# Full-array matmuls in four column parts, Q's masked copies in one op, and a fifth pair: a two-layer transformer block on one Trainium2 core

## The chip, the cores and the metric

The kernel runs on one core of a Trainium2 chip. The metric is the device time of one execution in microseconds (us); smaller is better. The kernel before takes 1614.82 us in the median of six runs (1612.02 to 1617.56). The engines of the core are called here as the profile calls them: PE (TensorE: matmuls; PEld is its loading of weights), DVE (VectorE), ACT (ScalarE), POOL (GpSimd) and SP (SyncE, which only issues DMAs here). Matmul results land in PSUM, of which the kernel uses eight banks of 128 partitions by 512 f32.

## The reference

```python
def _A_ref(x, wqkv, wo):                 # attention, 32 heads of 16
    qkv = (x @ wqkv).reshape(B, S, 3, H, Dh).transpose(2, 0, 3, 1, 4)
    q, k, v = qkv[0], qkv[1], qkv[2]
    scores = jnp.einsum("bhqd,bhkd->bhqk", q, k) * (Dh ** -0.5)
    p = _softmax(scores, axis=-1)
    o = jnp.einsum("bhqk,bhkd->bhqd", p, v)
    return o.transpose(0, 2, 1, 3).reshape(B, S, D) @ wo
...
x = x + _A_ref(_layernorm(x), A_wqkv, A_wo)
x = x + _B_ref(_layernorm(x), B_w1, B_w2)      # relu(x @ w1) @ w2
x = x + _A_ref(_layernorm(x), A_wqkv, A_wo)
x = x + _B_ref(_layernorm(x), B_w1, B_w2)
```

S is 2048, D 512, the hidden width of B 1792, and all inputs are bf16. The same weights serve both layers. With heads of 16 the scores are many and thin: 2 layers x 32 heads x 2048 x 2048, each of which wants one exp.

## The kernel before

**Tiles.** Queries go in chunks of 512 columns (QS); layer 1 takes its last two chunks as four of 256. Keys go in 16 blocks of 128 (kb). Eight heads lie in the 128 partitions of one key tile T, two heads in each strip g of 32 partitions. A unit of the attention is one head, one key block and one chunk of queries: a score matmul (L1302) with 32 contraction rows writes 128 keys x 512 queries into a PSUM bank. Since a strip holds two heads, Q exists in two copies, in each of which the other head's rows are zero; `q_masked` (L624 to L628) makes them out of a bank with one op for each e (0, 1). A score matmul uses the rows of one strip (tile position (32g, 0)), so that three of them, with different g, run beside each other.

**Slots.** Three banks (W = 3) form a slot: three units, three score matmuls side by side, and one exp on ACT over all three banks (L1311, 128x1536, bf16 result in one of five buffers `ebuf`). There are two sets of three banks (`ps_s`), one bank `ps_o` for the sums of values, and one, `ps_f`, for all other matmuls. The values' products (L901) contract 128 keys into 32 output rows: four of them, with different g, use the four column strips of the array (tile position (0, 32g)) and add into `ps_o`. A `vaug` block has a column of ones beside each head's values, so that the softmax sums come along; they are divided out later (L828 to L836).

**Pairs.** DVE computes some of the exps itself. In two slots, two apart, it takes the third bank instead of ACT, whose exp is then 128x1024 wide. `dve_block` (L991) copies such a bank as integers into half of a buffer `lin` (L995, step 1), and `chain` (L1031) works on both halves: bits kept (L1036), squared (L1047), bits kept again (L1036), multiplied (L1051; some pairs have one more step, L1048). The value products are then made three times, with `lin`, `step` and `cube`. There are NP = 4 buffers `lin` and NC = 3 of `step` and `cube`. A new pair begins only while fewer than NP are in flight, counted from the oldest that still has value products to make (L1200), and only where the planner's estimate of DVE's backlog (L1208) and of when its chain would end (L1207, L1217) allow it.

**The rest of the work.** Layer norm, K, Q, V, the output projection, and the two products of block B are groups of full-array matmuls, cut into pieces by `mm_group` (L418 to L441). A piece is one matmul of 128x128 weights by 512 or 256 columns (L434). When a group's last piece is out, DVE empties the bank: `k_fin`, `v_group`, `q_group`, `h_group` and others give the op. The transposes of layer norm (L516) are groups of a single piece with a cost of 1.3. Layer norm's reciprocal root is begun on DVE (`ln_rstd`, L473 to L480) and refined on POOL (`ln_newton`, L498 to L503), in buffers `va_`, `ya_`, `ta_` of which there are two of each.

**The order.** It is written by a planner in the kernel's own Python, which keeps a clock for PE and one for DVE. For each slot it places pieces of groups (`fill_pe`), rounds of value products (`fill_v`) and then the score matmuls (L1297 to L1307), before the time at which the exp before would end. If a slot has too little PE work, the score matmuls are issued again (`times`, L1293). `pe_start` (L257) adds SWITCH = 105 ns when the kind of PE work changes: "s" (scores), "v" (values), "f" (all else). The DVE queue is filled by `run_dve` in this rank: step 1 of a pair, emptying a bank, other tasks, chains. The order of each engine's instructions is thus fixed in the program. Q for the run after next is requested when a run's first unit comes up (L1181 to L1186) and lies in one of two buffers `qbuf`.

**Head and tail.** Before the first slot the first chunk's layer norm, K, Q and V are made with all engines (L1071 to L1117). After the last slot the last chunk's projection and block B remain (L1368 to L1438).

Of the kernel before, what the change touches and what calls it, by code (L numbers as in the profile page):

```python
# [24 lines left out]
def kernel(  # L25
# [41 lines left out]
    UNIT = 128.0  # L67
    EXP_BIAS = (127.0 - math.log2(SUM)) * UNIT
    CHAIN = 2500.0
    NP = 4  # L70
    NC = 3
    THIRD = (8, 9, 10, 11)

# [27 lines left out]
        return persist.tile(shape, dt, name=name)  # L101

    ident = sb([P, P], BF16, "ident")
    mask = [sb([P, 1], FP32, f"mask{e}") for e in range(2)]
    qmask = [sb([P, 1], FP32, f"qmask{e}") for e in range(2)]
    wqkv = sb([P, NDC, 3 * D], BF16, "wqkv")
    wo = sb([P, NDC, D], BF16, "wo")
    w1buf = [sb([P, NDC, P], BF16, f"w1_{n}") for n in range(NW1)]
# [38 lines left out]
    acc0 = [x[:].bitcast(FP32).rearrange("p a b -> p (a b)") for x in htp]  # L147
    acc0.append(kt1[:].bitcast(FP32).rearrange("p a b -> p (a b)"))
    ebuf = [sb([P, W * QS], BF16, f"e{n}") for n in range(NE)]
    qbuf = [[sb([P, QS], BF16, f"q{n}_{e}") for e in range(2)] for n in range(2)]  # L150
    ubuf = [sb([P, QS], FP32, f"u{n}") for n in range(NU)]
    rbuf = [sb([P, QS], FP32, f"r{n}") for n in range(NU)]
    cbuf = [sb([P, QS // 32], FP32, f"c{n}") for n in range(NU)]
    xnbuf = [sb([P, D], BF16, f"xn{n}") for n in range(TPC)]
    stats = [sb([P, nc.vector.BN_STATS_DIM], FP32, f"stats{n}") for n in range(2)]
    mv = [sb([P, TPC, nc.vector.BN_AGGR_DIM], FP32, f"mv{n}") for n in range(2)]
    va_ = [sb([P, TPC], FP32, f"va{n}") for n in range(2)]
    ya_ = [sb([P, TPC], FP32, f"ya{n}") for n in range(2)]
    ta_ = [sb([P, TPC], FP32, f"ta{n}") for n in range(2)]
    warm = sb([P, 1], FP32, "warm")  # L160

    ps_s = [psum.tile([P, W, QS], FP32, name=f"ps_s{n}") for n in range(2)]
# [80 lines left out]
    def at(keys, engine):  # L243
# [10 lines left out]
            t = max(t, when)  # L254
        return t

    def pe_start(kind, ready=0.0):  # L257
        return max(now_pe[0] + (SWITCH if mode[0] != kind else 0.0), ready)

    def pe_run(kind, units, ready=0.0):  # L260
        now_pe[0] = pe_start(kind, ready) + units * MM
# [38 lines left out]

    def do_piece():
        c, fn, ready = cur.popleft()
        pe_run("f", c, ready)
        fn()
        owed[0] -= c

# [111 lines left out]
    def mm_group(mms, fin, makes, deps, per=1, cost=EVAC, after=None, wide_by=QS, sums=1):  # L418


        hold = {}
        pieces = []
        n = len(mms)
        for a in range(0, n, per):

            def piece(a=a):
                if a == 0:
                    hold["b"] = bank()[:, 0 : sums * wide_by]
                b = hold["b"]
                for i in range(a, min(a + per, n)):  # L430
                    lhsT, rhs = mms[i]
                    k = n // sums
                    out = b[:, i // k * wide_by : (i // k + 1) * wide_by]
                    nc.tensor.matmul(out, lhsT, rhs, start=i % k == 0, stop=i % k == k - 1)  # L434
                if a + per >= n:
                    put_evac(cost, lambda: fin(b))
                    if after:
                        after()

            pieces.append((min(per, n - a) * wide_by / QS, piece))  # L440
        return group(pieces, makes, deps)  # L441
# [51 lines left out]
    def ln_newton(tag):  # L493

        n = ln_n(tag)
        a, y, t1 = va_[n][:], ya_[n][:], ta_[n][:]
        for _ in range(3):
            nc.gpsimd.tensor_mul(out=t1, in0=y, in1=y)  # L498
            nc.gpsimd.tensor_mul(out=t1, in0=t1, in1=a)
            nc.gpsimd.tensor_scalar(  # L500
                out=t1, in0=t1, scalar1=-0.5, scalar2=1.5, op0=ALU.mult, op1=ALU.add
            )
            nc.gpsimd.tensor_mul(out=y, in0=y, in1=t1)  # L503
# [117 lines left out]
            (wqkv[:, c, T * P : (T + 1) * P], xnT[xj][:, c, a : a + w]) for c in range(NDC)  # L621
        ]

    def q_masked(n, b, e, w=QS):  # L624
        return nc.vector.tensor_scalar(  # L625
            out=qbuf[n % 2][e][:, 0:w], in0=b, scalar1=qmask[e][:, 0:1], scalar2=None,
            op0=ALU.mult,
        )  # L628

    def q_group(n, l, j, T):  # L630
        xj, _, w = columns(l, j)
        cost = 133 + 1.045 * w

        def fin(b):
            q_masked(n, b, 0, w)
            evac.appendleft((cost, 0.0, lambda: (q_masked(n, b, 1, w), mark(("q", n)))))

        return mm_group(
            q_mms(l, j, T), fin, [("q", n)], each(TPC, "xnT", ("ln1", l, xj)), cost=cost,
            wide_by=w,  # L640
        )
# [151 lines left out]
    def finish_segment(sg, last):  # L793
        l, j, t, e = sg["l"], sg["j"], sg["t"], sg["e"]
        sums_wait[0] += 1
        if sg["store"] is not None:

            def store():
                if sg["load"] is not None:
                    nc.vector.tensor_add(out=sg["store"], in0=sg["load"], in1=ps_o[:])  # L800
                else:
                    nc.vector.tensor_copy(out=sg["store"], in_=ps_o[:])
                mark(("po",))
                sums_wait[0] -= 1

            musts.append((EVAC, now_pe[0] + PE_TO_DVE, store))
            return
        n = norm_no[0]
        norm_no[0] += 1
        if n >= NU:  # L810
            run_until(("m", n - NU))
        u, r, c = ubuf[n % NU], rbuf[n % NU], cbuf[n % NU]
        lane = DH if e == 0 else DH - 1
        width = sg["w"]
        at_column = columns(l, j)[1]
        sums = u[lane : P : 32, 0:width]
        c = c[:, 0 : width // 32]

        def copy():
            if sg["load"] is not None:  # L820
                nc.vector.tensor_add(out=u[:], in0=sg["load"], in1=ps_o[:])
            else:
                nc.vector.tensor_copy(out=u[:, 0:width], in_=ps_o[:, 0:width])  # L823
            mark(("po",))
            mark(("u", n))
            sums_wait[0] -= 1
            if sg not in segs[-2:]:
                nc.sync.dma_start(out=c, in_=sums)  # L828
                mark(("c", n), lag=C_LAG)

        musts.append((77 + 1.045 * width, now_pe[0] + PE_TO_DVE, copy))
        b = before(l, j)
        war = each(chunks[b][1], "o", *b) if b else []

        def mul(a, w):
            nc.vector.scalar_tensor_tensor(  # L836
                out=ot[t][:, at_column + a : at_column + a + w], in0=u[:, a : a + w], scalar=mask[e][:, 0:1],
                in1=r[:, a : a + w], op0=ALU.mult, op1=ALU.mult,
            )
            for i in range(a // P, (a + w) // P):  # L840
                mark(("ot", l, j, t, i))

        ended[l, j] = ended.get((l, j), 0) + 1
        quick = sg["load"] is not None or ended[l, j] == NT

        def recip():
            nc.vector.reciprocal(out=c, in_=c)
            nc.sync.dma_start(out=sums, in_=c)
            if not quick:
                nc.gpsimd.dma_start(  # L850
                    out=r[:, 0:width],
                    in_=bass.AP(
                        tensor=sums.tensor, offset=sums.offset,
                        ap=[list(sums.ap[0]), [0, 32], [1, width]],
                    ),
                )
            mark(("r", n), lag=U_LAG if quick else R_LAG)

        def spread():
            nc.vector.stream_shuffle(  # L860
                out=r[:, 0:width], in_=u[:, 0:width], mask=[lane] * 32
            )

        def spread_mul():
            if quick:
                spread()
            mul(0, width)

        def direct(i):
            if i == 0:  # L870
                spread()
            a = i * P
            nc.vector.reciprocal(out=r[:, a : a + P], in_=r[:, a : a + P])
            mul(a, P)

        def direct_all():
            for i in range(width // P):
                direct(i)

        ots = each(width // P, "ot", l, j, t)  # L880
        if last:
            last_steps.append(direct)
        elif sg is segs[-2]:
            task(3100, direct_all, ots + [("m", n)], war + [("u", n)])
        else:
            task(165, recip, [("r", n)], [("c", n)], place=0)
            cost = 105 + 1.1 * width + (200 + 1.05 * width if quick else 0)
            task(cost, spread_mul, ots + [("m", n)], [("r", n)] + war)
        if ended[l, j] == NT and not last:
            later = rest_of_chunk(l, j)  # L890
            work.extend(later)
# [180 lines left out]
    idle_matmuls(18)  # L1072
    for e in range(2):
        nc.vector.tensor_reduce(
            out=mask[e][:],
            in_=ident[:].rearrange("p (g e d) -> p e g d", g=4, e=2)[:, e],
            op=ALU.add, axis=mybir.AxisListType.XY,
        )
        nc.vector.tensor_scalar(
            out=qmask[e][:], in0=mask[e][:], scalar1=SCALE * LOG2E * UNIT, scalar2=None,  # L1080
            op0=ALU.mult,
        )
    for i in range(TPC):
# [24 lines left out]
    uses(nc.scalar.copy(out=ktp[0][0][0][:], in_=b), in_bank[0])  # L1108
    mark(("k", 0, 0, 0))
    b = plain(q_mms(0, 0, 0))  # L1110
    for e in range(2):
        uses(q_masked(0, b, e), in_bank[0])
    mark(("q", 0))
    for kb in range(2):
        b = plain(v_mms(kb))
# [57 lines left out]
    while units:  # L1173
# [123 lines left out]
        for _ in range(times):  # L1297
            pe_run("s", 1, s_ready)
            for a, (sg, kb, g) in sorted(zip(place, now), key=in_turn):
# [2 lines left out]
                nc.tensor.matmul(  # L1302
                    b[:, a : a + sg["w"]],
                    kt[32 * g : 32 * g + 32, kc : kc + P],
                    qbuf[sg["n"] % 2][sg["e"]][32 * g : 32 * g + 32, 0 : sg["w"]],
                    start=True, stop=True, tile_position=(32 * g, 0),
                )  # L1307
        m = len(now) - len(taken)
# [160 lines left out]
```

The softmax here doesn't subtract the row's maximum and nothing guards it: scores larger than these inputs give would overflow.

## Time and profile before

| | |
|---|---|
| profiled execution | 1614.79 us |
| its span in the profile | 1613.0 us |
| median of six runs | 1614.82 us |
| busy: ACT / DVE / PE | 1566.1 / 1496.7 / 1483.5 us |
| exps (L1311) | 1366 |
| step 1 of pairs (L995) | 662 |
| Q's masked copies (L625) | 102, and 2 in the head |
| value products (L901) | 6792 |
| full-array products (L434) in `ps_f` | 1576 |
| first exp starts, last exp ends | 16.7 us, 1578.1 us |
| granted clock of TensorE, mean | 0.998 |

The span runs from the first instruction to the last; the execution's own time is 1.8 us longer. A group in the profile is named by line, engine, operation and tiles (result <- operands, buffer numbers left out), then the shapes and the count; behind the bar stand the time in which at least one of its instructions ran, the mean duration of one in ns, and the idle time of the engine just before them with what ended it. Instructions of one engine overlap at their ends, so the distance between two starts is shorter than a duration. "x" before a number is a count. Line numbers are those of the kernel before.

### The profile page before, as it was taken

The page shows a single profiled execution, that of the slowest core. Times are in us where ns is not written, and L with a number is a line of the kernel's source. Part 1 is how long each engine was busy: PE and PEld are TensorE (multiplying, and loading weights), DVE is VectorE, ACT ScalarE, POOL GpSimd, SP SyncE. Part 2 cuts the span into 40 slices and gives each one's busy share as a digit, 9 for nine tenths or more (in the row PEclk, how much of TensorE's full clock was granted, in tenths as well). Part 3 has the DMA queues.
Part 4 walks back from the last instruction along what each step waited for, and adds up shares of the span by engine and source line. Part 5 has one row for each costly group of instructions (what it writes and reads, how often), then busy time and mean ns, then how long its engine had stood idle before and what let it go on. Part 6 is the DMA issues. An engine that isn't in the chain of part 4 may idle for free.

```text
span 1613.0 us, 35448 instructions
## 1 busy us (share of the span) xinstructions
PE 1483.5 (92%) x14863; PEld 508.6 (32%) x14863; DVE 1496.7 (93%) x3007; ACT 1566.1 (97%) x1387; POOL 94.0 (6%) x279
## 2 busy tenths in 40 slices
PE   8888889999999999999999999888999999999997
PEld 3222222322222222222222222222233333343444
DVE  7669999999999999999898998999999999999993
ACT  6999999999999999999999999999999999999993
POOL 2000001001010010000100000001001010010100
PEclk9999999999999999999999999999999999999999
DMA  5000000210002100021000100000110111021222
GB/s 164 1 1 2 2 2 8 47 28 10 7 15 44 25 15 8 12 48 25 9 1 17 30 1 1 2 3 10 43 30 16 27 28 38 19 49 37 47 48 70
DMA packets 113889, 39.97 MB, mean 25 GB/s; under 512 B 103328, under 2 KB 111264, under 8 KB 113728
## 3 DMA queue, kind: packets, MB, share of 16 engines
q1 hardware_dynamic: 101696, 26.21, 7.1%
q0 software_dynamic: 10688, 10.18, 3.4%
q8 instruction: 116, 1.90, 0.5%
q10 hardware_dynamic: 1344, 1.31, 0.2%
q14 instruction: 45, 0.37, 0.1%
HBM read 24.38 MB, written 2.10 MB: 16 GB/s over the span
## 4 chain that ended last, share of the span: by engine, by line
ACT 75%; PE 13%; DVE 8%; issue 3%; DMA 1%; ACTq 0%; DVEq 0%
ACT e L1311 75%; PE ps_s L1302 4%; PE ps_f L434 4%; PE ps_o L901 4%; DVE lin L995 2%; DVE step L1036 1%; DVE cube L1047 1%; PE ps_s L1365 1%; DVE cube L1051 1%; DVE stats L465 0%; DVE ot L836 0%; DVE x L708 0%; DMA w<-in_B_w_dram 0%; DVE ht L682 0%; DVE q L625 0%
## 5 line engine op out<-in xcount | busy, mean ns | idle before, releaser
L1311 ACT ACTIVATE e<-ps_s 128x1024 bf16<-128x1024 f32 (+1 forms) x1366 | 1555.0, 1370 | 6.8 <-PE ps_s L1302 4.9
L1302 PE MATMUL ps_s<-q,ktp 32*128 32x512 bf16 (+1 forms) x6060 | 600.6, 340 | 91.5 <-ACT e L1311 74.7
L901 PE MATMUL ps_o<-e,vaug 128*32 128x512 bf16 (+1 forms) x4284 | 495.1, 345 | 10.3 <-DVE u L823 4.8
L995 DVE TENSOR_SCALAR lin<-ps_s 128x512 int16<-128x512 f32 x662 | 451.3, 685 | 35.7 <-PE ps_s L1302 30.1
L1302 PEld LDWEIGHTS <-ktp 32*128 32x128 bf16 x6060 | 189.5, 91 | 505.1 <-issue 376.1
L1036 DVE TENSOR_SCALAR step<-lin 128x1024 int16<-128x1024 int16 x662 | 261.7, 418 | 3.3 <-PE ps_o L901 0.6
L901 PEld LDWEIGHTS <-vaug 128*32 128x32 bf16 x6004 | 161.6, 94 | 302.0 <-issue 291.1
L1047 DVE TENSOR_TENSOR cube<-step 128x1024 f16<-128x1024 bf16 x331 | 225.0, 683 | 2.7
L1051 DVE TENSOR_TENSOR cube<-cube,lin 128x1024 bf16<-128x1024 f16 x331 | 224.5, 679 | 0.0
L901 PE MATMUL ps_o<-step,vaug 128*32 128x512 bf16 (+1 forms) x836 | 143.1, 340 | 0.0
L901 PE MATMUL ps_o<-cube,vthird 128*32 128x512 bf16 (+1 forms) x788 | 138.1, 337 | 0.0
L901 PE MATMUL ps_o<-lin,vaug 128*32 128x512 bf16 (+1 forms) x836 | 127.4, 338 | 4.1 <-DVE u L823 2.8
L434 PE MATMUL ps_f<-xnT,w 128*128 128x512 bf16 (+1 forms) x496 | 126.8, 349 | 2.3 <-DVE ht L682 1.1
L434 PE MATMUL ps_f<-w,ht 128*128 128x512 bf16 x392 | 119.7, 384 | 0.9 <-DVE q L625 0.3
L850 POOL DMA_DIRECT2D r<-u x52 | 37.5, 722 | 1166.1 <-DVE step L1036 415.9
L434 PE MATMUL ps_f<-xnT,wqkv 128*128 128x512 bf16 (+1 forms) x328 | 92.0, 362 | 3.6 <-DVE ktp L575 0.5
L434 PE MATMUL ps_f<-wo,ot 128*128 128x512 bf16 x240 | 73.3, 387 | 0.5 <-DVE x L648 0.4
L682 DVE TENSOR_SCALAR ht<-ps_f 128x512 bf16<-128x512 f32 x103 | 70.5, 684 | 3.2 <-PE ps_f L434 3.0
L625 DVE TENSOR_SCALAR q<-ps_f,qmask 128x512 bf16<-128x512 f32 (+1 forms) x102 | 64.6, 659 | 2.9 <-PE ps_f L434 2.8
L434 PEld LDWEIGHTS <-w 128*128 128x128 bf16 x504 | 39.1, 97 | 60.0 <-issue 50.6
L836 DVE SCALAR_TENSOR_TENSOR ot<-u,mask,r 128x512 bf16<-128x512 f32 (+2 forms) x82 | 51.2, 626 | 1.1
L901 PEld LDWEIGHTS <-vthird 128*32 128x32 bf16 x788 | 39.8, 95 | 33.0 <-issue 30.3
(91 smaller groups left out, 612.1 us busy)
## 6 DMA issues: line engine op xcount, KB each, us to landing
w<-in_B_w_dram SPq DMA_DIRECT2D x140, 128.0 KB
r<-u POOLq DMA_DIRECT2D x25, 256.0 KB, 7.1
r<-u POOLq DMA_DIRECT2D x27, 128.0 KB, 4.5
out_dram<-x SPq DMA_DIRECT2D x16, 128.0 KB
x<-in_A_x_dram SPq DMA_DIRECT2D x14, 128.0 KB
w<-in_B_w_dram SPq DMA_DIRECT2D x1, 1792.0 KB
wqkv<-in_A_wqkv_dram ACTq DMA_DIRECT2D x2, 512.0 KB
c<-u SPq DMA_DIRECT2D x48, 8.0 KB
```

Source lines behind the costliest of these rows:

```text
L434: nc.tensor.matmul(out, lhsT, rhs, start=i % k == 0, stop=i % k == k - 1)
L625: return nc.vector.tensor_scalar(out=qbuf[n % 2][e][:, 0:w], in0=b, scalar1=qmask[e][:, 0:1], scalar2=None, op0=ALU.mult,)
L682: nc.vector.tensor_scalar(out=out, in0=sums, scalar1=0.0, scalar2=None, op0=ALU.max)
L836: nc.vector.scalar_tensor_tensor(out=ot[t][:, at_column + a : at_column + a + w], in0=u[:, a : a + w], scalar=mask[e][:, 0:1], in1=r[:, a ...
L850: nc.gpsimd.dma_start(out=r[:, 0:width], in_=bass.AP(tensor=sums.tensor, offset=sums.offset, ap=[list(sums.ap[0]), [0, 32], [1, width]],),)
L901: nc.tensor.matmul(ps_o[32 * g : 32 * g + 32, 0 : sg["w"]], values[:, 4 * sg["T"] + g, 2 * e : 2 * e + 32], rhs, start=g not in sg["begun" ...
L995: first = nc.vector.tensor_scalar(out=lin[which][:, half * QS : (half + 1) * QS], in0=src, scalar1=EXP_BIAS, scalar2=0.0, op0=ALU.add, op1 ...
L1036: nc.vector.tensor_scalar(out=stair, in0=line, scalar1=keep, scalar2=put, op0=ALU.bitwise_and, op1=ALU.bitwise_or,)
L1047: (609, lambda: nc.vector.tensor_mul(out=power, in0=mantissa, in1=mantissa)),
L1051: (609, lambda: nc.vector.tensor_mul(out=power.bitcast(BF16), in0=power, in1=line.bitcast(BF16))),
L1302: nc.tensor.matmul(b[:, a : a + sg["w"]], kt[32 * g : 32 * g + 32, kc : kc + P], qbuf[sg["n"] % 2][sg["e"]][32 * g : 32 * g + 32, 0 : sg[" ...
L1311: ex = nc.scalar.activation(out=eb[:, 0 : place[m]], in_=b[:, 0 : place[m]], func=ACTF.Exp, scale=1.0 / (LOG2E * UNIT),)
```

## The change

Five edits go together.

1. Each piece of `mm_group` issues its matmul as four, of 32 weight columns and 32 output rows each, at the tile positions that the value products use.
2. The planner's table of kinds (`MODE`) has "v" and "f" as one kind and gives the transposes a kind "t" of their own.
3. Q's two masked copies are one op: the bank read twice, times a [128, 2] tile of masks spread over the columns. Both copies lie in one tile `qbuf[n]`, both masks in one tile `masks`. Its estimated cost goes from two of 133 + 1.045 w to one of 90 + 2.09 w.
4. NP goes from 4 to 5: a fifth buffer `lin`, and a fifth pair in flight.
5. The two buffers of each of `va`, `ya` and `ta` become halves of one tile.

```diff
-    NP = 4
+    NP = 5
...
-    mask = [sb([P, 1], FP32, f"mask{e}") for e in range(2)]
-    qmask = [sb([P, 1], FP32, f"qmask{e}") for e in range(2)]
+    masks = sb([P, 4], FP32, "masks")
+    mask = [masks[:, e : e + 1] for e in range(2)]
+    qmask = masks[:, 2:4]
...
-    qbuf = [[sb([P, QS], BF16, f"q{n}_{e}") for e in range(2)] for n in range(2)]
+    qbuf = [sb([P, 2, QS], BF16, f"q{n}") for n in range(2)]
...
-    va_ = [sb([P, TPC], FP32, f"va{n}") for n in range(2)]
+    va2 = sb([P, 2, TPC], FP32, "va")
+    va_ = [va2[:, n] for n in range(2)]
...
+    MODE = {None: 0, "s": 1, "v": 2, "f": 2, "t": 3}
+
     def pe_start(kind, ready=0.0):
-        return max(now_pe[0] + (SWITCH if mode[0] != kind else 0.0), ready)
+        return max(now_pe[0] + (SWITCH if MODE[mode[0]] != MODE[kind] else 0.0), ready)
...
-        pe_run("f", c, ready)
+        pe_run("t" if c == 1.3 else "f", c, ready)
...
-                    nc.tensor.matmul(out, lhsT, rhs, start=i % k == 0, stop=i % k == k - 1)
+                    for g in range(4):
+                        cols = slice(32 * g, 32 * g + 32)
+                        nc.tensor.matmul(
+                            out[cols], lhsT[:, cols], rhs, start=i % k == 0,
+                            stop=i % k == k - 1, tile_position=(0, 32 * g),
+                            skip_group_check=True,
+                        )
...
-    def q_masked(n, b, e, w=QS):
-        return nc.vector.tensor_scalar(
-            out=qbuf[n % 2][e][:, 0:w], in0=b, scalar1=qmask[e][:, 0:1], scalar2=None,
-            op0=ALU.mult,
+    def q_masked(n, b, w=QS):
+        return nc.vector.tensor_mul(
+            out=qbuf[n % 2][:, :, 0:w],
+            in0=b.rearrange("p (e q) -> p e q", e=1).to_broadcast((P, 2, w)),
+            in1=qmask.rearrange("p (e q) -> p e q", q=1).to_broadcast((P, 2, w)),
         )
...
-        cost = 133 + 1.045 * w
+        cost = 90 + 2.09 * w
 
         def fin(b):
-            q_masked(n, b, 0, w)
-            evac.appendleft((cost, 0.0, lambda: (q_masked(n, b, 1, w), mark(("q", n)))))
+            q_masked(n, b, w)
+            mark(("q", n))
...
-                    qbuf[sg["n"] % 2][sg["e"]][32 * g : 32 * g + 32, 0 : sg["w"]],
+                    qbuf[sg["n"] % 2][32 * g : 32 * g + 32, sg["e"], 0 : sg["w"]],
```

`ya` and `ta` change as `va` does. The matmuls of the head (L1069, L1103), the transposes (L516) and the tail's own products (L1365) stay as they are.

## The prediction

> **What bounds the kernel now.** I read the page's chain first, then the groups by shape, then busy time by stage, and last the timeline of the engines around one slot. The chain, and the group that carries it:
>
> ```profile
> ACT 75%; PE 13%; DVE 8%; issue 3%; DMA 1%; ACTq 0%; DVEq 0%
> ...
> L1311 ACT ACTIVATE e<-ps_s 128x1024 bf16<-128x1024 f32 (+1 forms) x1366 | 1555.0, 1370 | 6.8 <-PE ps_s L1302 4.9
> ```
>
> ScalarE (ACT) runs 1366 exps that cover 1555.0 of the 1613.0 us, with 6.8 us idle before them. The other 58 us are the head (the first exp starts at 16.7), the tail (the last ends at 1578.1) and little else. So the time moves if the exps get fewer columns or start closer together. The groups by shape:
>
> ```profile
> L1311 ACT ACTIVATE e<-ps_s 128x1536 bf16<-128x1536 f32 x703 | 1053.5, 1577 | 4.3 <-PE ps_s L1302 2.6 <-PE ps_o L901 1.2
> L1311 ACT ACTIVATE e<-ps_s 128x1024 bf16<-128x1024 f32 x662 | 719.2, 1151 | 2.5 <-PE ps_s L1302 2.3 <-PE ps_o L901 0.2
> ...
> L995 DVE TENSOR_SCALAR lin<-ps_s 128x512 int16<-128x512 f32 x662 | 451.3, 685 | 35.7 <-PE ps_s L1302 30.1
> ```
>
> The 662 narrow exps are the slots whose third bank VectorE (DVE) takes at L995: 331 pairs. Neighbouring instructions overlap, so I price by distances between starts in the timeline: 1.330 us after a wide exp, 0.904 after a narrow one (medians). **One more pair saves 2 x 0.426 = 0.85 us of ACT.** All exps at these paces are 703 x 1.330 + 662 x 0.904 = 1533 us, while they span 1561: about 27 us are late starts. In the timeline 23 exps over 0.1 us late make 9.1 us of that; the rest is some 13 ns on nearly every exp, which I expect to stay.
>
> How much room has DVE for pairs? Busy time by stage (columns: window, PE, PEld, DVE, ACT, POOL, granted clock, DMA):
>
> ```profile
> 200.00:300.00 100.00, 89.16 (x785) 26.47 (x780) 95.34 (x189) 98.02 (x89) 4.74 (x14) 0.97 0.06 12
> ...
> 500.00:600.00 100.00, 93.96 (x773) 27.88 (x771) 98.24 (x190) 100.00 (x92) 4.73 (x11) 1.00 0.13 27
> ...
> 900.00:1000.00 100.00, 94.36 (x786) 29.36 (x783) 90.94 (x174) 99.63 (x89) 3.78 (x12) 1.00 0.03 8
> ```
>
> Best stages are 98% busy, the one at 900 only 91%. From 100 to 1560 us DVE is busy 1395.4 of 1460: 64.6 us are idle. That idle time, and what the change frees on DVE, is the purse.
>
> **All full-array products in four column parts.** The timeline of PE (start, us, line) shows both forms and the switch:
>
> ```profile
> 802.73 0.39 PE L901 MATMUL ps_o<-lin,vaug 128*32 128x512 bf16 x1
> 803.06 0.82 PE L434 MATMUL ps_f<-wqkv,xnT 128*128 128x512 bf16 x3
> 803.81 0.39 PE L1302 MATMUL ps_s<-q,ktp 32*128 32x512 bf16 x3
> ```
>
> ```profile
> 154.96 0.62 PE L901 MATMUL ps_o<-e,vaug 128*32 128x512 bf16 x8
> 155.40 0.39 PE L901 MATMUL ps_o<-lin,vaug 128*32 128x512 bf16 x4
> 155.72 0.39 PE L1302 MATMUL ps_s<-q,ktp 32*128 32x512 bf16 x3
> ```
>
> A value round followed by a full product takes 0.33 us from start to start. Full product to full product is (0.82 - 0.39) / 2 = 0.215. Two value rounds of four column products take 0.44, so 0.22 each, eight instructions included. A change of form thus costs about 0.105, and a full product cut in four should cost what a value round does. Following the rows of PE, a value round meets a full product 606 times one way and 65 the other: 671 x 0.105 = 70 us of PE go. L434 has 392 + 336 + 264 + 240 + 120 = 1352 wide products and 224 of 256 columns; at 0.01 us more for each that gives back at most 16 us. Transposes keep the full form; a cut product beside one now pays a switch, at most once for each of 64, 7 us. The planner's table MODE drops the same switch, so its order counts on it. The 3 x 1576 added products and as many weight loads are in that round price. PE is 92% busy, not the bound, so its 47 to 70 us reach the time only through late exps. 9.1 us are there to win; about 3 of them fall at 235 to 242 us, where the clock was granted at 0.5, and others are DVE's. I take 1.5 us; the ends are 0 and 9.
>
> No row shows four column products that read the same moving operand. The nearest is the value round, whose four read different blocks; its worst form, four after one another, is 3 x 0.215 more per wide product and half that for the others, 945 us in all. I take the value round, since shape, tile and bank use are the same.
>
> The Trainium skill, "TensorEngine Tiling (Array Packing)", section Restrictions and Gotchas, speaks against the edit: column tiling excludes Fast Weight Load. This trace does not show that as a price: the value products' weight loads last 94 ns on average against 97 for full ones, and whole rounds keep 0.22 us. If the four loads ran one after another instead, a product would take 4 x 0.094 = 0.38 us and the edit would cost 1576 x 0.16 = 250 us of PE; by the rounds it costs nothing.
>
> **Q's masked copies in one op.** Today two TENSOR_SCALARs at L625 (two start at 17.11 us and last 1.41 together: 0.66 from start to start), 0.40 each for the 256 form. The new op reads 1024 elements. L823 takes 683 ns for 512 and 417 for 256 elements of f32, 1.04 ns per element; a two-operand op of 512 (L648, 681) holds DVE for 0.60, so one of 1024 holds it 0.60 + 0.53 = 1.13. For 256 columns it is 0.60. Saved: 1.32 - 1.13 = 0.19, and 0.20. With 51 runs: 51 x 0.19 = 9.7 us of DVE. Ends: at the slope of L836 (747 and 468, 1.09 per element, start distance 0.67) it is 1.22, saving 5 us; at the rate of the 16-bit L1047 (1024 in 0.60) it would save some 31. The source is f32 in PSUM, so I take 9.7. A pair costs DVE 2 x 0.60 (L995) + 2 x 0.33 (L1036) + 0.60 (L1047) + 0.60 (L1051) = 3.06. So 9.7 / 3.06 = 3.2 pairs, **-2.7 us**, where the planner spends it on pairs. The single op delays a step 1 queued behind it on DVE by up to 1.13 instead of 0.66, 51 times; the scores wanted next are two slots ahead, so I price that in the third rival. In the head the first scores wait for both copies, but stand behind L434 at 15.53 anyway: nothing.
>
> **A fifth pair.** A pair holds its lin buffer from its first L995 to its last L901 product on cube. Counted so, pairs live 13.8 us in the median, 4 are in flight for 31% of 100 to 1560 us, 3 for 50%, and half of all pairs begin within 3.2 us of the end of the fourth pair before, where 2.1 is about the least seen. So NP gates about half the starts; NC does not (L1047 starts 6.4 us, median, after the third pair before has ended). Of the 64.6 us of DVE idle 12.2 lie at 4 in flight and 24.6 at 3, where the planner's gate can hold as well. The remaining 28 lie at 2 or fewer, where other gates (keys, values, the end of a segment) decide. I take 15 us as won: 15 / 3.06 = 4.9 pairs, **-4.2 us**. Ends: nothing, and all 64.6 (21 pairs, -18).
>
> **The shared tiles.** va, ya and ta of two chunks now lie in one tile each: a chunk's L473 could wait for the POOL steps of the chunk before, 12 x 0.28 = 3.4 us at worst. There are 16 such chunks, mostly tens of us apart, so nothing; one meeting costs 3.4 of DVE. q's one tile waits for both heads of two runs before, whose scores were issued before the four products that come first: nothing, or a slot of 1.1 us if that order breaks.
>
> **The sum** against the profiled execution (1614.79, span 1613.0, 1.8 around it; the runs' median is 1614.82, the same): -2.7 - 4.2 - 1.5 = -8.4, so **1606.4, said as 1607**. What is late next is DVE: at about 97% of the middle stages.
>
> **Rivals.**
> 1. *The idle time is filled nearly whole.* (64.6 + 9.7) / 3.06 = 24 pairs, -20.6: 1594. For it: nearly all idle gaps end on PE (scores, evacuations), which becomes lighter. Against: 28 us lie where NP is no gate. Chance 0.15.
> 2. *The gate is only passed on.* The condition on queued chains counts each pair in flight, and refuses the fifth; Q's saving stays: about 1612, no change. DVE at 98% in the stages from 300 to 600 speaks for it. Chance 0.18.
> 3. *Slower: DVE's queue gets late for the scores.* Score weight loads already wait for DVE:
>
> ```profile
> PEld L1302 <- DVE step L1036: 38.8, 102, 0.4
> PEld L1302 <- DVE lin L995: 23.9, 70, 1.3
> PEld L1302 <- DVE cube L1047: 15.2, 40, 0.4
> PEld L1302 <- DVE cube L1051: 12.4, 32, 0.4
> ```
>
> These 90 us now mostly end inside ACT's current exp. With a quarter more chains in flight and longer Q ops I price a fifth more, 18 us; if all of it reaches the exps: 1614.8 - 2.7 - 4.2 + 18 = 1626. It decides from 6.9 us of added lateness, 5 ns per exp. Chance 0.18.
> 4. *The cut products are not one round.* PE has its 129 us of idle and 70 of switches, and from about (129 + 70) / 1576 = 0.13 us more per product it binds; four in a row give 1614.8 + 945 - 199 = 2361. PE at 92% and the missing row speak for it, the value rounds against. Chance 0.04.
>
> The forecast has 0.45. **Chances:** faster by over 0.2% (below 1611.6; about what a measurement can tell) 0.45 + 0.15 = 0.60, within 0.2% 0.18, slower 0.18 + 0.04 = 0.22. **Range** 1594 to 1626: from the first rival's time to the third's; outside remain some of each and the fourth. The forecast's own range is 1600 to 1611.
>
> **What would show it.** Right: consecutive value rounds and quarters 0.22 apart with no 0.33 between them; a Q op of about 1.2 us, 51 times; L995 above 662, say 678; the narrow exps as many; DVE above 1500 us busy; ACT's idle before exps not above 6.8. Wrong: L995 near 662 (rival 2); more late exps with DVE behind them (3); quarters spaced wider than 0.22 (4); more stretches of granted clock 0.5 like the one at 235 us, which cost about 3 us.

## The result and the profile after

The changed kernel takes 1608.22 us in the median of 20 runs (1603.73 to 1616.05), the kernel before 1614.05 (45 runs). The ratio is 0.9964, 95% interval 0.9955 to 0.9972: 5.8 us or 0.36% faster, where 1607 had been forecast.

The page's group of exps and four groups by shape of the kernel after (columns as before):

```profile
L1323 ACT ACTIVATE e<-ps_s 128x1536 bf16<-128x1536 f32 (+1 forms) x1366 | 1548.6, 1368 | 16.9 <-PE ps_s L1314 11.2
```

```profile
L1323 ACT ACTIVATE e<-ps_s 128x1536 bf16<-128x1536 f32 x685 | 1028.9, 1578 | 8.3 <-PE ps_o L914 4.3 <-PE ps_s L1314 3.6
L1323 ACT ACTIVATE e<-ps_s 128x1024 bf16<-128x1024 f32 x680 | 735.1, 1157 | 8.1 <-PE ps_s L1314 7.1 <-PE ps_o L914 0.8
...
L1008 DVE TENSOR_SCALAR lin<-ps_s 128x512 int16<-128x512 f32 x680 | 462.9, 684 | 34.5 <-PE ps_s L1314 28.8
...
L637 DVE TENSOR_TENSOR q<-ps_f,masks 128x1024 bf16<-128x1024 f32 x35 | 42.6, 1218 | 3.5 <-PE ps_s L1314 1.7 <-PE ps_f L442 1.6
```

Step 1 went from 662 to 680: nine pairs more, and as many slots that moved from the wide exps to the narrow ones. Q's op lasts 1218 ns. But ACT's idle time before the exps rose from 6.8 to 16.9 us, and this profiled execution took 1616.05 us, the slowest of all 20: its mean granted clock is 0.987, while the execution of 1603.73 us was granted 0.996. The clock is listed with each execution, and within the changed kernel the time rises by some 1.3 us for each 0.001 that it falls (a straight line through the 21 listed). The kernel before loses 1.1 us per 0.001, but has a median clock of 0.996 against 0.992 (its runs beside the experiments).

So I split the span into terms that can be read from any trace: the head (to the first exp), the pace (wide exps x 1.330 + narrow ones x 0.904), small lateness (under 0.1 us an exp), large lateness, and the tail (from the end of the last exp). Lateness is how much further apart two exps end than the pace says.

| us, profiled execution | pairs | head | pace | small | late | tail | span |
|---|---|---|---|---|---|---|---|
| before | 331 | 16.7 | 1533.9 | 18.2 | 9.2 | 34.9 | 1613.0 |
| after | 340 | 18.0 | 1526.3 | 17.5 | 21.0 | 31.3 | 1614.2 |

The pace is 7.6 shorter, as nine pairs at 0.85 should make it. The tail is 3.6 shorter, although its first 4.7 us ran at half clock. The lateness is 11.8 longer, and 13.0 of its 21.0 lies in and just behind stretches of half clock. So this one execution is 1.2 us longer than the one of before; the gain of 5.8 us is one of the medians. Two of these stretches, from 154.0 to 167.7 and from 222.3 to 232.6 us, cost 10 us of exps. Busy time just before the first and in it (window, PE, PEld, DVE, ACT, POOL, clock, DMA), and how it began on DVE and PE:

```profile
150.00:154.00 4.00, 2.21 (x25) 0.60 (x18) 3.83 (x7) 4.00 (x5) 0.00 (x0) 1.00 0.00 0
154.00:168.00 14.00, 12.90 (x84) 2.68 (x84) 8.74 (x18) 8.10 (x7) 0.00 (x0) 0.51 0.02 2
```

```profile
150.40 1.22 DVE L637 TENSOR_TENSOR q<-ps_f,masks 128x1024 bf16<-128x1024 f32 x1
...
152.15 0.72 DVE L873 STREAM_SHUFFLE r<-u 128x512 f32<-128x512 f32 x1
...
152.91 0.75 DVE L849 SCALAR_TENSOR_TENSOR ot<-u,masks,r 128x512 bf16<-128x512 f32 x1
153.57 0.69 DVE L1008 TENSOR_SCALAR lin<-ps_s 128x512 int16<-128x512 f32 x1
154.18 0.68 DVE L1064 TENSOR_TENSOR cube<-cube,lin 128x1024 bf16<-128x1024 f16 x1
154.32 0.61 PE L1314 MATMUL ps_s<-q,ktp 32*128 32x512 bf16 x3 [1.25 <-DVE lin L1008]
```

DVE works through the long Q op, a step 1 and the two ops of a division (152.15 and 152.91); the next step 1 starts late, at 153.57, and the next scores, which overwrite its bank, wait 1.25 us for it. PE is busy 2.21 of 4 us, and then its clock is granted at 0.51 for the next 14 us, in which ACT is busy 8.1. That is the third rival's mechanism (DVE late for the scores), and the half clock behind it lasts longer than the thin stretch that led to it. The second stretch begins in the same way: scores wait 0.95 us for a step 1 before 222.37.

The cut products did what their step said. The timeline of PE after (start, us, line):

```profile
701.11 0.40 PE L914 MATMUL ps_o<-e,vaug 128*32 128x512 bf16 x4
701.33 0.82 PE L442 MATMUL ps_f<-xnT,w 128*32 128x512 bf16 x12
702.09 0.39 PE L1314 MATMUL ps_s<-q,ktp 32*128 32x512 bf16 x3
...
703.34 0.40 PE L914 MATMUL ps_o<-e,vaug 128*32 128x512 bf16 x3
703.36 1.25 PE L442 MATMUL ps_f<-xnT,w 128*32 128x512 bf16 x16
```

From a value round to the cut products behind it there are 0.22 us, no longer 0.33, and three products in twelve parts take (0.82 - 0.39) / 2 = 0.215 each. Behind a round of three values (703.34) the first quarter starts 0.02 us later, in the free strip. That saves nothing by itself here: the next scores start at 704.53, which is five rounds of 0.215 us and one change of form (0.105) after 703.34.

### The profile page after: what moved, and what is told of

It reads as the page before. It is cut to its first block, busy times and chain, and to the rows that moved or that the text cites. A ratio compares the mean times of both kernels' runs of the same rounds, so it can differ in the third digit from the quotient of the medians.

```text
span 1614.2 us, 45384 instructions
## 1 busy us (share of the span) xinstructions
PE 1452.8 (90%) x19833; PEld 543.1 (34%) x19833; DVE 1506.3 (93%) x3012; ACT 1558.5 (97%) x1385; POOL 93.0 (6%) x279
## 5 line engine op out<-in xcount | busy, mean ns | idle before, releaser
L1323 ACT ACTIVATE e<-ps_s 128x1536 bf16<-128x1536 f32 (+1 forms) x1366 | 1548.6, 1368 | 16.9 <-PE ps_s L1314 11.2
L1314 PE MATMUL ps_s<-q,ktp 32*128 32x512 bf16 (+1 forms) x6192 | 616.8, 343 | 112.5 <-ACT e L1323 97.4
L1008 DVE TENSOR_SCALAR lin<-ps_s 128x512 int16<-128x512 f32 x680 | 462.9, 684 | 34.5 <-PE ps_s L1314 28.8
L442 PE MATMUL ps_f<-xnT,w 128*32 128x512 bf16 (+1 forms) x2016 | 147.5, 345 | 6.4 <-DVE ht L695 3.7
L442 PE MATMUL ps_f<-w,ht 128*32 128x512 bf16 x1624 | 147.1, 381 | 1.7 <-DVE q L637 0.7
L442 PE MATMUL ps_f<-xnT,wqkv 128*32 128x512 bf16 (+1 forms) x1312 | 107.7, 366 | 3.5 <-DVE vaug L623 1.9
L442 PE MATMUL ps_f<-wo,ot 128*32 128x512 bf16 x960 | 87.1, 381 | 1.5 <-DVE x L661 0.7
L442 PEld LDWEIGHTS <-w 128*32 128x32 bf16 x2016 | 58.3, 96 | 36.9 <-issue 19.0
L637 DVE TENSOR_TENSOR q<-ps_f,masks 128x1024 bf16<-128x1024 f32 (+1 forms) x51 | 53.6, 1050 | 4.6 <-PE ps_s L1314 2.6
L442 PEld LDWEIGHTS <-ht 128*32 128x32 bf16 x1624 | 47.0, 96 | 27.4 <-issue 12.2
L849 DVE SCALAR_TENSOR_TENSOR ot<-u,masks,r 128x512 bf16<-128x512 f32 (+2 forms) x82 | 51.0, 624 | 1.1
```

The lines of the kernel that those rows point to most:

```text
L442: nc.tensor.matmul(out[cols], lhsT[:, cols], rhs, start=i % k == 0, stop=i % k == k - 1, tile_position=(0, 32 * g), skip_group_check=True,)
L637: return nc.vector.tensor_mul(out=qbuf[n % 2][:, :, 0:w], in0=b.rearrange("p (e q) -> p e q", e=1).to_broadcast((P, 2, w)), in1=qmask.rear ...
L849: nc.vector.scalar_tensor_tensor(out=ot[t][:, at_column + a : at_column + a + w], in0=u[:, a : a + w], scalar=mask[e], in1=r[:, a : a + w] ...
L1008: first = nc.vector.tensor_scalar(out=lin[which][:, half * QS : (half + 1) * QS], in0=src, scalar1=EXP_BIAS, scalar2=0.0, op0=ALU.add, op1 ...
L1314: nc.tensor.matmul(b[:, a : a + sg["w"]], kt[32 * g : 32 * g + 32, kc : kc + P], qbuf[sg["n"] % 2][32 * g : 32 * g + 32, sg["e"], 0 : sg[" ...
L1323: ex = nc.scalar.activation(out=eb[:, 0 : place[m]], in_=b[:, 0 : place[m]], func=ACTF.Exp, scale=1.0 / (LOG2E * UNIT),)
```

## The experiments

Twelve kernels, each timed beside the kernel before; a result is given as the ratio to it with its 95% interval, then the median. Theories: **A**, the gain is the added pairs alone; **B**, what PE saves reaches the exps by itself; **C**, cut products make the clock fall; **D**, formed after the first four: the gain is PE's room, without which a fifth pair and the long op make DVE and PE late for each other; **E**, one place near 1190 us decides between orders. The terms of all profiled executions stand in the table after the last experiment.

**split_same_order.** The loop over g of the diff alone, in the kernel before.

> The cut products alone, with the planner's kinds, Q and NP as before, so every engine's order is that of before. Theory A (the gain is the added pairs at 0.85 us each; what PE saves is not on the path; more stretches of half clock gave part of it back because slots are left thin): 331 pairs, 0 to 2 us faster, 1612 to 1614, granted clock as before, about 0.998. Theory B (PE's saved switches reach the exps directly): 4 to 9 us faster, 1605 to 1610. Theory C (four column products count for less activity than one full product, so that the clock falls): clock at or below 0.993 and 3 us or more slower. If a cut product cost more than a round of 0.22 us, PE would be busier than 1483 us.

0.9992 (0.9979 to 1.0004), 1612.40 us, median clock 0.996: no difference that can be told. PE is busy 1449.0 us for 1483.5, although 22 us of this execution ran at half clock and only 7 of the one of before. So 34.5 us of PE buy at most 3.4 us while the order stays (against B, which gave them 4 to 9), and cut products do not by themselves lower the clock to 0.993 (against C).

**split_and_plan.** The same, with MODE and the kind "t".

> Cut products and the planner's table of kinds; Q in two ops and NP 4 as before. Theory A: the planner finds about 4 pairs more, so 3.4 us less, given back in part by the clock if thin slots come from the planner running ahead: 1611 to 1614. Theory B: 1605 to 1610. Theory C: as in the run with the order of before, clock at or below 0.993.

0.9962 (0.9946 to 0.9978), 1607.14 us. The planner, which now knows that values and products need no switch, found 3 pairs (2.5 us of pace) and emptied the tail: 34.9 to 27.9. That is as much as the whole change gains. The tail of the kernel before, on PE:

```profile
1578.45 1.05 PE L434 MATMUL ps_f<-xnT,w 128*128 128x256 bf16 x8
1579.33 1.04 PE L434 MATMUL ps_s<-xnT,w 128*128 128x256 bf16 x8
1580.20 3.19 PE L434 MATMUL ps_s<-w,ht 128*128 128x512 bf16 x14
```

These 30 products of block B were left over when the last exp ended at 1578.1, 5 us of PE with nothing beside it. In split_and_plan, and in each of the other seven kernels with the common kind, none is left; the new orders without it leave 26 to 74. No run has the planner's table with full products, so that the new order needs the cut products is likely, since the planner counts on the switches that they save, but not shown.

**q_only.** The changed kernel with full products, MODE without the common kind, NP = 4.

> Q's two copies in one op and the shared tiles, everything else as before. The prediction gave this 9.7 us of DVE and 3.2 pairs. Theory A: the freed time is not turned into pairs, since NP holds the starts (one pair fewer by the program's own order): 1613 to 1616. If the prediction's step is right: 1611 to 1612 and 668 of step 1. A rival: the op of 1.2 us makes the steps queued behind it late, so that it is slower by more than 3 us.

1.0032 (1.0019 to 1.0045), 1618.96 us: slower. DVE is busy 1488.2 for 1496.7, so the 9.7 us were nearly there (8.5), but not one pair came of them: 331. What made it slower is settled in part: the median clock fell from 0.996 to 0.9935, some 3 us, and 4.5 us of exps are late between 1180 and 1210 us, where the kernel before loses 1.8. There DVE's queue stands 2.78 us for a DMA of the softmax sums, and PE waits 3.00 us behind it; that is not the rival's reason, the long op.

**fifth_only.** `NP = 5`, shared tiles, Q in two ops, full products.

> NP 5 alone, with the shared tiles, Q in two ops into one tile, full products and the planner's kinds as before. Theory A: about 8 more pairs, 8 x 0.85 = 6.8 us less, 1607 to 1609, clock as before: the fifth pair is all of the gain. Theory B: 2 to 4 us less, the rest needs PE's relief. A rival (DVE fuller, scores late): 1614 or above.

1.0129 (1.0108 to 1.0151), 1635.46 us, clock 0.981 to 0.987. It has 339 pairs, eight more, and 6.8 us less of pace, and is 20.5 us slower. Waits in its trace (waiter <- what ended the wait: us, times, longest):

```profile
PEld L1308 <- DVE lin L1001: 30.0, 78, 3.6
...
ACT e L1317 <- PE ps_s L1308: 17.3, 27, 2.7
...
PE ps_s L1308 <- DVE lin L1001: 7.7, 8, 3.1
```

```profile
1185.99 0.25 DVE L853 RECIPROCAL c<-c 128x16 f32<-128x16 f32 x1 [3.50 <-DMA c<-u]
```

Before, the first stood at 23.9, 70, 1.3, the second at 4.9, 13, and the third at 2.4, 5. Scores wait for steps 1, and the exps for the scores. The longest of each of the three waits (3.6, 2.7, 3.1) is one and the same place, near 1187 us: DVE had stood 3.50 us at a RECIPROCAL for a DMA, with step 1 queued behind it. Without that place the three are still 26.4, 14.6 and 4.6 us. There are five stretches of half clock, and 54 products are left for the tail. Theory A fell here.

**no_split.** The whole change except edits 1 and 2.

> The whole change without the cut products and without the planner's common kind: Q in one op, NP 5, full products. Theory D (formed after the first four runs: the gain is PE's room; without it a fifth pair and the long Q op make PE and DVE late for each other, thin the slots, drop the clock and leave work behind the last exp): slower than before, 1625 to 1640, clock 0.980 to 0.988, though it has 7 pairs more. Theory A (pairs alone): 1608 to 1610.

1.0060 (1.0043 to 1.0077), 1624.74 us, 338 pairs. Slower, as D says, though at a clock of 0.994, where I had expected less: 26.9 us of lateness are enough. Of these 8.0 lie between 1180 and 1210 us, where DVE stands 4.37 us for a DMA of the softmax sums. Against the changed kernel, edits 1 and 2 are worth some 16 us here, and 6 to 8 in the kernel before (split_and_plan).

**split_fifth.** The changed kernel with Q in two ops.

> Cut products, the common kind and NP 5, but Q in two ops. 9 pairs more than before. Theory D with a useless Q op: as the changed kernel or 1 to 3 us better, 1604 to 1608, since the op of 1.2 us no longer stands before a step 1. If the Q op is what the change needs: 1609 or more.

1.0018 (1.0007 to 1.0028), 1617.75 us with 340 pairs: 9.5 us slower than the changed kernel, against what I expected. Most of it is two places close together. The first, in the timeline:

```profile
1180.86 0.25 DVE L859 RECIPROCAL c<-c 128x16 f32<-128x16 f32 x1 [2.75 <-DMA c<-u]
...
1181.90 0.68 DVE L833 TENSOR_TENSOR u<-vaug,ps_o 128x512 f32<-128x512 f32 x1
...
1182.63 0.62 PE L913 MATMUL ps_o<-e,vaug 128*32 128x512 bf16 x4 [2.56 <-DVE u L833]
...
1183.85 1.02 ACT L1323 ACTIVATE e<-ps_s 128x1024 bf16<-128x1024 f32 x1 [2.51 <-PE ps_s L1314]
```

DVE's queue stands 2.75 us at a RECIPROCAL whose DMA has not landed (issued at 1173.57; the planner reckons 3.6 us). The copy out of `ps_o` queues behind it, the value products behind that, then the scores, then ACT. That makes 3.8 us of late exps. The second place follows, and no DMA holds it up:

```profile
1190.99 2.77 PE L442 MATMUL ps_f<-w,ht 128*32 128x512 bf16 x48
...
1193.81 0.69 DVE L720 TENSOR_TENSOR x<-x,ps_f 128x512 bf16<-128x512 bf16 x1 [2.77 <-PE ps_f L442]
...
1196.98 1.45 ACT L1323 ACTIVATE e<-ps_s 128x1536 bf16<-128x1536 f32 x1 [5.53 <-PE ps_o L913]
```

Twelve products stand in a row there. DVE waits 2.77 us to empty their bank, with the last step of a chain queued behind, the value products wait for that chain, and an exp that needs its buffer back starts 5.53 us late. Between 1180 and 1210 us 10.0 us of exps are late, against 2.1 in the kernel after and 1.8 before.

**split_q.** The changed kernel with NP = 4.

> The changed kernel with NP 4: cut products, common kind, Q in one op. Theory D (the fifth pair's gain is eaten by the clock): within 3 us of the changed kernel, 1605 to 1611, with 333 pairs and a clock not below 0.993. Theory A: 7 pairs fewer than the changed kernel, so 6 us slower, 1613 to 1615.

0.9981 (0.9966 to 0.9996), 1610.57 us, 332 pairs, clocks from 0.985 to 0.998. Between these two orders the fifth pair is thus worth 2 to 3 us, where eight pairs would be 6.8.

**floor_62.** The changed kernel with more repeats of the scores:

```diff
-    FLOOR = 0.56
+    FLOOR = 0.62
```

> The changed kernel with FLOOR 0.62 for 0.56: the planner repeats score matmuls in more of the thin slots (about 6650 for 6340 of them by the program's order); it has 340 pairs as well. Theory D: the clock rises to 0.996 or more and gives back most of what half clock took, 1600 to 1605. If the clock is not what eats the gain: 1607 to 1612, the repeats being in the way or nothing.

0.9907 (0.9885 to 0.9928), 1598.43 us, median clock 0.998 with runs up to 0.999. The groups of exps and of step 1 in its trace:

```profile
L1323 ACT ACTIVATE e<-ps_s 128x1536 bf16<-128x1536 f32 x683 | 1023.7, 1571 | 6.1 <-PE ps_s L1314 5.8
L1323 ACT ACTIVATE e<-ps_s 128x1024 bf16<-128x1024 f32 x682 | 733.6, 1143 | 4.5 <-PE ps_s L1314 4.3
...
L1008 DVE TENSOR_SCALAR lin<-ps_s 128x512 int16<-128x512 f32 x682 | 463.1, 684 | 26.7 <-PE ps_s L1314 20.5 <-ACT e L1323 0.7
```

One pair more than the kernel after, 6769 score matmuls in the trace for 6192, and 9.8 us faster. Not all of that is the clock. Two of its six executions, the profiled one among them (17.1 us of half clock in one stretch), were granted 0.992 and took 1604.4 us; the four of the kernel after at 0.992 took 1608.0 to 1610.6. So 4 to 6 us of the 9.8 remain at the same clock, and belong to the other order and the one pair more.

**split_fifth_lag.** split_fifth with longer estimates for the two DMAs of the softmax sums:

```diff
-    C_LAG, R_LAG, U_LAG = 3600.0, 10500.0, 3000.0
+    C_LAG, R_LAG, U_LAG = 6500.0, 10500.0, 5000.0
```

> The run with cut products, fifth pair and Q in two ops (1617.75 us), with the planner's estimate of the two small DMAs of the softmax sums raised: C_LAG from 3.6 to 6.5 us, U_LAG from 3 to 5. Theory E (its loss against the changed kernel is one place: from 1178 to 1199 us DVE's queue stands behind a RECIPROCAL that waits for the sums' DMA, and 10 us of exps are late there): that place shrinks to 3 us or less, so 1609 to 1612, with 338 pairs. If the loss comes from Q's two ops all along the kernel: still 1616 or more.

0.9917 (0.9904 to 0.9931), 1600.56 us. At 1203 us 0.8 us of exps are late, instead of 10 between 1180 and 1210, and the whole lateness fell from 25.9 to 6.5 us. That is more than the place itself: the order changed elsewhere too, and the median clock rose from 0.991 to 0.996. Both the wait for the DMA and the row of twelve products are gone, so the run does not show that the estimate was the cause of either. Q in two ops is no handicap here.

**before_floor_62.** FLOOR 0.62 in the kernel before.

> The kernel before with FLOOR 0.62 alone; 331 pairs. Theory D (more repeats hold the clock, and PE's room for them comes from the cut products): the clock rises to 0.999, but it was 0.997 already, so 0 to 4 us are won, 1610 to 1614, or lost if the repeats stand before value rounds. If FLOOR is worth 10 us by itself: 1604 or less.

1.0095 (1.0081 to 1.0109), 1629.44 us, at a clock of 0.997. I had expected a loss only if the repeats stood before value rounds. The repeats push products behind the last exp (74 are left, the tail is 43.3 us), and lateness rises to 15.8. The kernel before has no room on PE for them; the changed one has.

**split_and_plan_floor_62.** FLOOR 0.62 in split_and_plan.

> Cut products and the common kind with FLOOR 0.62; NP 4, Q in two ops, 332 pairs. Theory D (half clock takes 4 to 8 us, the fifth pair gives 0.85 us a pair once the clock is held): 1602 to 1606, that is 5 to 8 us slower than the changed kernel with FLOOR 0.62 (1598.4), with the clock at 0.997 or above. If the fifth pair and the one Q op are worth nothing even then: 1599 or less.

0.9950 (0.9936 to 0.9963), 1605.39 us, 332 pairs, clock 0.998. At the same median clock floor_62, with NP 5 and the one Q op, is 7.0 us faster, and its nine pairs more are 7.7 at 0.85. But that is the difference of two orders: the next run has the same two edits, 341 pairs and the same clock, and is 1.0 us slower than this one.

**floor_62_lag.** Both edits, FLOOR and the estimates, in the changed kernel.

> The changed kernel with FLOOR 0.62 and with the raised estimates of the two DMAs; about 341 pairs. Theories D and E together: 1594 to 1598, faster than both kernels and at or below the run with FLOOR 0.62 alone, where some 2.6 us of exps are late around 1184 to 1189. If the estimates do not matter there: within 2 us of 1598.4, or slower if the order changes for the worse elsewhere.

0.9950 (0.9937 to 0.9962), 1606.35 us: 8 us slower than floor_62, at the same median clock. The longer estimates are no remedy as such; they made another order, with its own bad place, of the second kind of split_fifth, seen on PE:

```profile
1202.46 2.77 PE L442 MATMUL ps_f<-w,ht 128*32 128x512 bf16 x48
1206.63 0.40 PE L914 MATMUL ps_o<-cube,vthird 128*32 128x256 bf16 x4 [1.39 <-DVE cube L1064]
```

Twelve products stand in a row there again, the value products wait for a chain that waits behind them, and an exp that needs its buffer back starts 5.0 us late.

| profiled execution, us | pairs | pace | late | tail | median clock | median time |
|---|---|---|---|---|---|---|
| before | 331 | 1533.9 | 9.2 | 34.9 | 0.996 | 1614.05 |
| split_same_order | 331 | 1533.9 | 11.2 | 33.1 | 0.996 | 1612.40 |
| split_and_plan | 334 | 1531.4 | 14.2 | 27.9 | 0.993 | 1607.14 |
| q_only | 331 | 1533.9 | 10.4 | 34.8 | 0.994 | 1618.96 |
| split_q | 332 | 1533.1 | 10.7 | 28.0 | 0.994 | 1610.57 |
| fifth_only | 339 | 1527.1 | 25.6 | 40.3 | 0.982 | 1635.46 |
| no_split | 338 | 1528.0 | 26.9 | 33.6 | 0.994 | 1624.74 |
| split_fifth | 340 | 1526.3 | 25.9 | 28.0 | 0.991 | 1617.75 |
| after | 340 | 1526.3 | 21.0 | 31.3 | 0.992 | 1608.22 |
| split_fifth_lag | 338 | 1528.0 | 6.5 | 29.9 | 0.996 | 1600.56 |
| floor_62 | 341 | 1525.4 | 14.1 | 27.4 | 0.998 | 1598.43 |
| floor_62_lag | 341 | 1525.4 | 14.7 | 27.8 | 0.998 | 1606.35 |
| split_and_plan_floor_62 | 332 | 1533.1 | 6.8 | 28.2 | 0.998 | 1605.39 |
| before_floor_62 | 331 | 1533.9 | 15.8 | 43.3 | 0.997 | 1629.44 |

Pairs, pace, lateness and tail are of one execution, clock and time of all; a profiled execution can lie some us off its median.

## Why the prediction was right, and where it was not

The time, its side and its size were right: 1608.2 for 1607, -5.8 us for -8.4. That the time came so close is in part luck: the sum had two gains from pairs and a small one from lateness, while the runs show pairs and the tail as gains, a loss by lateness, and half clock that the sum had no term for. Two of the prediction's own signs of being wrong appeared beside those of being right: more late exps with DVE behind them, and more stretches of half clock. By its steps:

- **What bounds the kernel.** Right. The exps' pace is 94 to 96% of every span, and nine pairs took 7.6 us off it: 0.85 each.
- **A cut product costs a round, and the switch goes.** Right: 0.215 and 0.22 us. The fourth rival is out. PE was busy 34.5 us less in the order of before, where 47 to 70 were reckoned, with 15 us more of half clock in that execution.
- **Q's op.** The cost was right (1.13 us from start to start, as reckoned, at a duration of 1218 ns; DVE 8.5 us less busy for 9.7). That it turns into 3.2 pairs was wrong: alone it gave none, and a slower kernel.
- **The fifth pair.** 4.9 pairs were forecast; eight came, both alone and in the changed kernel (against split_q), and six beside Q in two ops (split_fifth against split_and_plan). The sum of both steps, 8.1 pairs, met the nine by luck: one too high, the other too low, and three come with the common kind alone (split_and_plan).
- **PE's saving reaches the time only through late exps, -1.5.** This is the mis-sized term, on two sides. The lateness did not fall, it rose by 11.8 us in the profiled execution; in the median less, since that execution had the lowest clock of all. And the tail, which I left out of the sum, fell by 3.6 (by 7 in split_and_plan).
- **The third rival (DVE late for the scores)** I gave 0.18 as a thing that happens or not. It did happen: alone, the fifth pair is 1.3% slower, 1635 us where the rival had 1626, in part by the DMA near 1187 us that no step had reckoned with. In the whole change edits 1 and 2 outweighed it. The step's error was to treat the parts as separate sums: without edits 1 and 2 the rest loses 10.5 us, with them the whole wins 5.8.

Each edit to the planner's numbers makes another order, and two such orders lie 8 us (floor_62 and floor_62_lag) or 17 us apart (split_fifth and split_fifth_lag), more than the whole change gains. A single pair of kernels could therefore differ by its orders alone. All runs together speak against that for edits 1 and 2: of the eight kernels with the common kind seven are faster than the kernel before (1598.4 to 1610.6 us) and one is slower, and all four new orders without it are slower (1619.0 to 1635.5). For Q's op and the fifth pair the runs decide no such thing.

What stays open: whether the planner's table alone, with full products, would do as well; why q_only's clock fell; and whether any estimate would keep the place near 1190 us quiet in all orders.

## What to carry to other kernels

When a planner writes the order, an edit is worth what the order can do with it: freed engine time bought nothing until the planner's own table knew of it, and a deeper pipeline alone lost 1.3%, in part at one DMA for whose landing its order left too little time. Price head, pace, lateness and tail each for itself, and give the granted clock a term of its own: a late instruction on one engine thins the work of TensorE, and in these traces a short thin stretch was paid for longer than it lasted (4 us of it at 150, then 13.7 us of half clock). Two versions of one kernel are compared by several edits of the order, not by one.

## What the runs showed of the hardware

- In the kernel after the clock fell to 0.5 behind thin stretches of PE, with no idle time over 1.3 us in them. Counting a full product of 512 columns as 0.213 us, a score matmul as a third of that and a column product as a quarter, PE streamed 0.25, 0.36, 0.44 and 0.37 of the 3.4 us before the four falls that this kernel had between its first and its last exp; 0.34 before the one of the kernel before. Other runs have falls behind idle time as well (no_split at 1193.8 us, where PE had stood 4.37 us; split_q at 1181.9, 3.32 us). Stretches as thin as 0.31 (the kernel before, 1126 us) and 0.24 (floor_62_lag, 1208 us) stayed at full clock, so this is no sharp bound. All falls that ended inside a span lasted multiples of 3.4 us (3.4, 6.8, 10.2, 13.7, 17.1).
- The same kernel, run again on the same data, is granted clocks from 0.987 to 0.996, and its times differ by 12 us.
- A round of one to three column products leaves other strips free, and the first quarter of a cut product starts in one of them 0.01 to 0.02 us after the round (medians for two and three), against 0.227 behind a round of four. No run shows that this shortens the kernel.
